# The gate as a tanh of half its argument, and a new order for the first third of a written-out list of steps

## The chip, the cores and the metric

The kernel runs on one core of one Trainium2 chip. The metric is the time of one launch in microseconds of the device; three runs of the kernel before took 293.01, 293.01 and 293.41 us, a median of 293.01 us.

## The reference

For 8 batches, 8 heads, 576 tokens and 64 channels a head, the reference computes a linear attention and feeds it to a gated layer. All is in float32.

```python
q_s = softmax(q, over the 64 channels of a head)
k_s = softmax(k, over the 576 tokens)
kv  = einsum('bhsd,bhse->bhde', k_s, v)          # 64x64 a head
x   = q_s @ kv, heads side by side               # (576, 512) a batch
gate = sigmoid(sum over 5 taps of conv_w[t] * x shifted by 4 - t tokens)   # per channel
out = (gate * (x @ w_val)) @ w_out
```

## The kernel before, in words

The 512 channels lie on the 128 partitions in four blocks, the 576 tokens along the free axis. The work is cut into named steps, one small function each, with a batch and a block as arguments: `tap 0 1 3` is the step `tap` (L546) of batch 0, block 1, tap 3. `ORDER` (L32) is a list of 969 steps written out by hand; the kernel walks down it and issues each step's instructions, so the list is the order on every engine's queue at once. A letter at a step's end names its engine (`a` ScalarE, `v` VectorE, `p` GpSimd). Nothing else moves an instruction: an engine takes its own steps in the order of the list and waits at each for what the step needs. All loads and stores (`load_*`, `put`, `k_row`, `k_spread`) are issued by SyncE, also in list order.

The steps of a batch, with the engine that does them:

- k: batches 0 and 1 load k by channels (`load_kc`, L314), take the maximum (`k_top`, VectorE), the exponential (`k_raise`, ScalarE) and turn it on TensorE (`k_turn`, `k_tail_turn`, copied out by `k_turned`, `k_tail_turned`). Later batches load it by tokens, take the maximum from a second copy (`load_km`, `k_peak`), spread it over the partitions through memory (`k_row`, `k_spread`), subtract it on GpSimd (`k_sub`, L298) and take the exponential (`k_exp`, `kt_exp`).
- q: maximum (`q_max`), subtraction (`q_sub`, GpSimd) and exponential (`q_exp`; `q_each` does both on ScalarE, eight heads one by one), sum (`q_sum`, with `q_eps` and `q_rec`), scaling (`q_mul`), turned on TensorE (`q_turn`, `tail_turn`, copied out by `q_turned`, `tail_turned`, `tail_high`).
- `kv`, `kv_sums`, `kv_norm`, then `attend`, which writes x of two blocks at a time into PSUM.
- the gate of one block: `first` scales x by the newest tap, `tap` adds one of the four others on VectorE straight from PSUM, or else `far` (ScalarE) writes the scaled block to SBUF and `near` (GpSimd) adds it; then `sigmoid` (L560).
- `x_high` and `x_low` split x in a rounded part and the rest; `value` (L584) multiplies both by the weights in 24 matmuls of 288 columns a half; `gated` (L588) multiplies the result in PSUM by the gate; `g_high`, `g_low` split that; `project` (L600) multiplies it by the second weights; `copy` (L609) brings it out of PSUM and `put` stores it.
- the weights arrive as 64-bit words and are converted once, in eight slabs (0 to 3 of `w_val`, with the conv taps, 4 to 7 of `w_out`): `part`, `field`, `scaled`, `signed`, `joined`, `taps`, `w_high`, `w_low`. `value b m` needs slab m, `project b n` slab 4 + n.

PSUM is cut into four equal buffers under one tag (`bank`, L152). Each of the four x blocks, each `value` and `project`, `kv` and each group of turned blocks takes one, and a new one takes the buffer whose last reader stands earliest in the list. SBUF tiles are shared in the same way (six buffers for k's second copies and the weights in conversion, two for stored output, two each for q, k and v).

ScalarE's functions need tables; the compiler puts an ACT_TABLE_LOAD ahead of an ACTIVATE whose function the tables in place do not have.

Of the kernel before, what the change touches and what calls it, by code (L numbers as in the profile page):

```python
# [51 lines left out]
    k_tail_turn 1, k_turn 1 1, field 7 p, first 0 2 a, q_eps 1 2 4 a, k_turned 1 0 a, tap 0 2 3, q_rec 1 2 4,
    k_tail_turned 1 a, q_rec 1 0 2, tap 0 3 3, w_high 4 a, q_mul 1 3 p, value 0 2, k_peak 2 0, g_high 0 1 a,
    q_mul 1 1 p, g_high 0 0 a, tap 0 3 2, k_turned 1 1 a, tap 0 2 2, q_mul 1 2 p, w_high 5 a, tap 0 3 1, g_low 0 0 p,
    q_mul 1 0 a, k_peak 2 3, kv 1, tap 0 2 1, k_row 2, g_low 0 1 p, tap 0 2 0, scaled 7 a, scaled 6 a, tap 0 3 0,
    w_low 5 p, sigmoid 0 2, q_turn 1 0, k_peak 3 3, load_k 2, load_kt 2, kv_sums 1, value 0 3, part 6 p, part 7 a,
    load_km 3 1, gated 0 2, kv_norm 1 a, load_vt 2, q_max 2 0 5, k_spread 2, g_high 0 2 p, q_turned 1 0 a, w_low 4 p,
    sigmoid 0 3, g_low 0 2 p, q_turn 1 1, gated 0 3, attend 1 0, signed 7, g_high 0 3 a, q_turned 1 1 a, signed 6,
    x_high 1 0 a, g_low 0 3 v, project 0 0, first 1 0 a, first 1 1 a, joined 6 p, tap 1 0 3, x_high 1 1 a, tap 1 0 2,
    joined 7 p, project 0 1, tap 1 0 1, copy 0 0 a a, w_high 6 a, put 0 0, x_low 1 0, w_high 7 a, load_km 3 0,  # L60
    w_low 6 p, tap 1 0 0, load_km 4 1, tap 1 1 3, w_low 7 p, load_km 5 0, tap 1 1 2, load_v 2, attend 1 1, copy 0 1 a a,
# [623 lines left out]
```

## Time and profile before

The profile is of one execution. Its span, first to last instruction, is 291.0 us; the launch takes about 2.0 us more (293.01 - 291.0).

| engine | busy us | share of the span | instructions |
|---|---|---|---|
| TensorE matmuls | 264.8 | 91% | 2544 |
| VectorE | 235.7 | 81% | 332 |
| ScalarE | 219.1 | 75% | 339 |
| GpSimd | 203.5 | 70% | 190 |

In 40 slices of the span (7.3 us each) TensorE is at nine tenths or more in all but the first six and the last; the first two are empty, the fourth and fifth are at seven and three tenths. VectorE, ScalarE and GpSimd are at seven to nine tenths from the second slice on. A group of instructions is a line of the kernel, an engine, an operation and its tiles, with the count, the busy time, the mean duration of one, and the idle time of the engine ahead of them with what ended it. Starts in a timeline are from the start of the span, and durations of neighbours on one engine overlap a little, so what one costs its engine is the distance from start to start.

### The profile page before, as it was taken

The numbers are of one execution on the slowest core, as the hardware profiler recorded it, in microseconds if no ns is written. First come the engines' busy times: TensorE is split into PE (matmuls) and PEld (weight loads), VectorE is DVE, ScalarE is ACT, GpSimd is POOL, SyncE is SP. The second block draws the span as 40 slices with busy tenths as digits, with TensorE's granted clock in tenths as the row PEclk, the third lists the DMA queues.
The fourth block names the chain that finished last, engine by engine and source line by source line (L and its number), as shares of the span: only waits on it lengthen the run. The fifth ranks groups of instructions, "written<-read, shape, count | busy, mean of one in ns | idle before, by whom it ended". The sixth has DMA issues, their size and how long they took to land.

```text
span 291.0 us, 6460 instructions
## 1 busy us (share of the span) xinstructions
PE 264.8 (91%) x2544; PEld 249.0 (86%) x2544; DVE 235.7 (81%) x332; ACT 219.1 (75%) x339; POOL 203.5 (70%) x190
## 2 busy tenths in 40 slices
...
GB/s 228 399 415 402 360 334 4 279 140 328 353 137 331 219 174 317 273 264 207 184 276 339 252 111 322 385 166 118 147 187 138 199 35 2 41 41 83 0 83 81
DMA packets 22158, 60.77 MB, mean 209 GB/s; under 512 B 3184, under 2 KB 3696, under 8 KB 19440
## 3 DMA queue, kind: packets, MB, share of 16 engines
...
## 4 chain that ended last, share of the span: by engine, by line
PE 84%; DVE 6%; ACT 4%; DMA 2%; SPq 1%; issue 1%; ACTq 0%
PE out L572 36%; PE val L572 33%; PE kv L466 6%; PE x L525 5%; DMA kc<-in_k_channels 2%; PE qTps L491 2%; ACT q L444 1%; DVE qs L376 1%; DVE qm L361 1%; DVE ktop L322 1%; DVE e L258 1%; DVE e L257 1%; ACT L561 0%; DVE kpk L286 0%; ACT gate L561 0%
## 5 line engine op out<-in xcount | busy, mean ns | idle before, releaser
L572 PE MATMUL val<-x,w_val_hi 128*128 128x288 f32 x512 | 90.6, 299 | 0.0
L549 DVE SCALAR_TENSOR_TENSOR gate<-x,cw,gate 128x574 f32<-128x574 f32 (+3 forms) x107 | 85.3, 806 | 5.0 <-ACT gate L538 1.9
L572 PEld LDWEIGHTS val<-x,w_val_hi 128*128 128x128 f32 x512 | 76.9, 192 | 0.0
L572 PE MATMUL val<-x,w_val_lo 128*128 128x288 f32 x256 | 57.1, 305 | 5.6 <-DVE gate L549 5.6
L572 PE MATMUL out<-gh,w_out_lo 128*128 128x288 f32 x256 | 56.8, 301 | 0.0
L572 PE MATMUL out<-gh,w_out_hi 128*128 128x288 f32 x256 | 55.5, 296 | 0.0
L572 PEld LDWEIGHTS val<-x,w_val_lo 128*128 128x128 f32 x256 | 41.7, 192 | 6.9 <-POOL w_val_lo L274 6.0
L572 PEld LDWEIGHTS out<-gh,w_out_lo 128*128 128x128 f32 x256 | 41.0, 188 | 5.8 <-issue 2.2
L598 POOL TENSOR_TENSOR gl<-g,gh 128x576 fp32r<-128x576 f32 x22 | 31.4, 1429 | 16.7 <-ACT gh L166 9.7
L166 ACT COPY o<-out 128x576 f32<-128x576 f32 (+1 forms) x29 | 17.9, 621 | 32.2 <-PE out L572 23.4
L572 PEld LDWEIGHTS out<-gh,w_out_hi 128*128 128x128 f32 x256 | 41.2, 188 | 0.0
L558 POOL TENSOR_TENSOR gate<-gate,far 128x572 f32<-128x572 f32 (+3 forms) x21 | 28.0, 1339 | 18.7 <-ACT far L554 10.8
L572 PE MATMUL out<-gl,w_out_hi 128*128 128x288 f32 x256 | 39.5, 295 | 0.0
L572 PEld LDWEIGHTS out<-gl,w_out_hi 128*128 128x128 f32 x256 | 35.9, 188 | 0.0
L590 DVE TENSOR_TENSOR g<-val,gate 128x576 f32<-128x576 f32 x32 | 24.1, 754 | 14.2 <-PE val L572 10.2
L366 POOL TENSOR_TENSOR q<-q,qm 128x512 f32<-128x512 f32 x31 | 32.3, 1063 | 2.4 <-issue 2.4
L301 POOL TENSOR_TENSOR k<-k,kmax 128x512 f32<-128x512 f32 x23 | 30.4, 1339 | 0.2
L544 DVE TENSOR_TENSOR x<-x,x 128x576 fp32r<-128x576 f32 x32 | 23.3, 749 | 2.9 <-ACT x L166 1.6
L435 POOL TENSOR_TENSOR qc<-qc,lb 128x576 f32<-128x576 f32 x13 | 19.1, 1480 | 8.9 <-DMA lb<-lrow 5.8
L561 ACT ACTIVATE gate<-gate 128x576 f32<-128x576 f32 x32 | 21.5, 684 | 0.9 <-DVE gate L549 0.6
L554 ACT ACTIVATE far<-x,cw 128x572 f32<-128x572 f32 (+3 forms) x21 | 15.4, 740 | 8.5 <-PE x L525 3.2
L166 ACT CAST x<-x 128x576 fp32r<-128x576 f32 x27 | 17.0, 642 | 6.0 <-PE x L525 4.3
...
## 6 DMA issues: line engine op xcount, KB each, us to landing
...
```

The costliest lines, as they stand in the source:

```text
L166: nc.scalar.copy(out=out, in_=in_)
L301: engine(e).tensor_sub(kk[r, cs], kk[r, cs], mx[r, cs])
L366: engine(e).tensor_tensor(qq, qq, m, op=ALU.add if b < 2 else ALU.subtract)
L435: engine(e).tensor_sub(t, t, T["lb", b][:, p])
L466: nc.tensor.matmul(acc[h * D:(h + 1) * D, p, :], T["k", b][:, c, cs] if c < 4 else ktz[b % 2][:, cs], T["v", b][:, c, hd] if c < 4 else T[ ...
L544: nc.vector.tensor_sub(xl, T["x", b, p], T["xh", b, p].bitcast(F32))
L549: nc.vector.scalar_tensor_tensor(out=a, in0=x, scalar=w, in1=a, op0=ALU.mult, op1=ALU.add)
L558: nc.gpsimd.tensor_add(a, a, T["far", b, p, j])
L561: nc.scalar.activation(T["gate", b, p], T["gate", b, p], AF.Sigmoid)
L572: nc.tensor.matmul(ps[:, cs], a[:, kb, ms], z[:, cs], start=(i == 0), stop=(i == len(parts) - 1))
L590: nc.vector.tensor_mul(T["g", b, m], T["val", b, m], T["gate", b, m])
L598: engine(e).tensor_sub(T["gl", b, m], T["g", b, m], T["gh", b, m].bitcast(F32))
```

## The change

Three functions: the gate becomes tanh(x/2) instead of sigmoid(x); `gated` multiplies the value by gate + 1 in one instruction with two operations instead of one multiplication; `copy` scales by 0.5 where it only copied. Together that is the same product. In `ORDER` the steps ahead of `q_mul 2 3 p` (317 before, 320 after) stand in another order, some on another engine, and three of batch 0's and 1's taps (`tap 0 1 2`, `tap 0 0 0`, `tap 1 0 0`) become a `far` and a `near` each. The first 22 loads keep their order. From `q_mul 2 3 p` on the two lists are the same, step by step (the diff shows some of these lines only for their line breaks).

```diff
-    load_words 3, load_q 0 2 5, load_q 0 1 2, load_words 0, load_kc 0 0, load_kc 0 2, load_ident, load_kc 0 3, part 3 a,
...
-    q_sub 0 1 p, q_exp 0 3 4, k_raise 0 2, k_top 0 3, part 0 p, load_km 2 2, load_words 2, k_raise 0 3, signed 0,
-    q_exp 0 2 3, k_top 0 1, k_raise 0 0, field 1 p, q_sum 0 2 5, q_exp 0 1 2, joined 0 p, k_raise 0 1, k_turn 0 0,
-    part 1 a, load_km 2 1, load_kc 1 0, load_kc 1 2, load_q 1 0 5, load_words 5, scaled 1 p, q_max 0 0 1, q_eps 0 2 5 p,
-    k_turn 0 1, signed 1, q_each 0 0, load_kc 1 3, q_rec 0 2 5, k_turned 0 0 v, q_mul 0 4 p, k_tail_turn 0,
-    k_turned 0 1 a, q_mul 0 3 p, q_sum 0 0 2, tail_turn 0, k_tail_turned 0 a, taps 3 p, joined 1 v, tail_turned 0 a,
-    kv 0, w_high 0 a, q_eps 0 0 2 v, field 2 p, q_rec 0 0 2, k_peak 2 2, tail_high 0 a, q_mul 0 1 a, q_mul 0 0 p,
-    k_top 1 0, k_peak 2 1, q_mul 0 2 p, q_turn 0 0, k_top 1 2, w_high 3 a, scaled 2 p, kv_sums 0, taps 1 a, taps 0 a,
-    part 2 p, q_turn 0 1, kv_norm 0 v, q_turned 0 0 a, signed 2, q_turned 0 1 a, attend 0 0, q_max 1 0 2, joined 2 p,
-    k_raise 1 2, attend 0 1, q_max 1 2 4, w_high 1 p, field 5 p, first 0 1 a, x_high 0 0 a, tap 0 1 3, first 0 0 a,
-    q_sub 1 0 p, k_top 1 3, x_high 0 1 a, taps 2 p, tap 0 0 3, w_low 1 p, k_raise 1 3, tap 0 1 2, scaled 5 a,
-    w_high 2 a, part 5 p, load_km 3 2, load_kc 1 1, load_words 4, load_words 6, load_k 4, load_km 2 0, x_low 0 1,
-    load_v 1, x_high 0 2 a, w_low 3 p, tap 0 1 1, x_high 0 3 a, k_raise 1 0, tap 0 1 0, q_sub 1 1 p, load_km 2 3,
...
-    k_top 1 1, w_low 2 p, tap 0 0 0, x_low 0 2, field 4 p, q_exp 1 0 1, x_low 0 3, value 0 1, k_raise 1 1, signed 5,
...
+    load_words 3, load_q 0 2 5, load_q 0 1 2, load_words 0, field 3 p, part 3 a, load_kc 0 0, scaled 3 a, signed 3,
...
+    load_words 1, q_sum 0 2 5, load_q 0 0 1, taps 3 p, scaled 0 a, q_sub 0 1 p, k_raise 0 2, k_top 0 1, k_top 0 3,
+    load_vt 0, q_exp 0 1 2, load_v 0, load_km 2 2, k_raise 0 0, load_words 2, q_eps 0 2 5 a, w_low 3 p, q_rec 0 2 5,
+    k_raise 0 1, k_turn 0 0, field 1 p, k_raise 0 3, part 1 p, q_max 0 0 1, load_km 2 1, scaled 1 a, k_turn 0 1,
+    signed 1, joined 1 v, q_each 0 0, k_turned 0 0 a, q_mul 0 4 p, k_tail_turn 0, q_sum 0 0 2, tail_turn 0, signed 0,
+    taps 1 p, load_kc 1 0, k_tail_turned 0 a, q_eps 0 0 2 a, q_rec 0 0 2, q_mul 0 2 p, tail_turned 0 v,
+    k_turned 0 1 a, load_kc 1 2, field 2 p, load_q 1 0 5, q_mul 0 1 a, q_mul 0 0 p, scaled 2 a, q_mul 0 3 p,
+    part 2 a, kv 0, q_turn 0 0, q_turn 0 1, tail_high 0 a, joined 0 p, k_top 1 0, k_peak 2 2, k_top 1 2, kv_sums 0,
+    q_turned 0 0 a, kv_norm 0 v, load_words 5, signed 2, attend 0 0, load_kc 1 3, load_km 3 2, joined 2 p,
+    q_turned 0 1 a, first 0 1 a, far 0 1 2, q_max 1 0 2, x_high 0 1 a, q_max 1 2 4, attend 0 1, field 5 p, k_top 1 3,
+    x_high 0 2 a, taps 2 p, taps 0 p, tap 0 1 3, x_high 0 0 a, load_km 2 3, tap 0 1 0, w_high 1 p, x_high 0 3 a,
+    first 0 0 a, w_high 0 p, q_each 1 3, load_kc 1 1, w_low 1 p, x_low 0 1, w_high 2 p, tap 0 1 1, x_low 0 0,
+    x_low 0 2, tap 0 0 2, first 0 3 a, load_v 3, first 0 2 a, q_sub 1 0 p, tap 0 0 1, w_low 0 p, tail_high 1 a,
+    k_raise 1 3, load_words 4, scaled 5 p, q_sub 1 1 p, near 0 1 2, k_raise 1 0, x_low 0 3, tap 0 0 3, far 0 0 0,
+    tap 0 2 2, value 0 1, load_v 1, load_words 6, load_words 7, q_exp 1 0 1, sigmoid 0 1, value 0 0, k_top 1 1,
+    w_low 2 p, k_raise 1 1, tap 0 2 1, q_exp 1 1 2, gated 0 1, near 0 0 0, k_turn 1 0, tap 0 2 3, field 4 p,
+    tap 0 2 0, load_km 2 0, scaled 4 p, k_raise 1 2, q_sum 1 0 2, signed 4, load_k 2, q_each 1 2, signed 5,
+    sigmoid 0 0, field 7 p, value 0 2, part 4 a, g_high 0 1 a, q_eps 1 0 2 a, gated 0 0, k_turned 1 0 a, q_rec 1 0 2,
+    k_tail_turn 1, q_sum 1 2 4, g_high 0 0 a, part 5 p, tap 0 3 2, q_eps 1 2 4 a, joined 4 p, value 0 3, sigmoid 0 2,
...
+    k_turn 1 1, load_q 2 0 5, k_peak 2 3, q_mul 1 3 p, g_low 0 1 p, joined 5 p, gated 0 2, q_mul 1 2 a, field 6 p,
+    tap 0 3 1, g_high 0 2 a, k_turned 1 1 a, q_turn 1 0, q_turned 1 0 a, scaled 7 a, q_max 2 0 5, part 6 a,
+    k_peak 2 1, kv 1, kv_sums 1, kv_norm 1 v, w_high 5 a, q_turn 1 1, g_low 0 2 p, sigmoid 0 3, attend 1 0,
...
-        nc.scalar.activation(T["gate", b, p], T["gate", b, p], AF.Sigmoid)
+        nc.scalar.activation(T["gate", b, p], T["gate", b, p], AF.Tanh, scale=0.5)
...
-        nc.vector.tensor_mul(T["g", b, m], T["val", b, m], T["gate", b, m])
+        nc.vector.scalar_tensor_tensor(out=T["g", b, m], in0=T["gate", b, m], scalar=1.0, in1=T["val", b, m], op0=ALU.add, op1=ALU.mult)
...
-        copied(e, T["o", b, n][:, piece(h)], T["out", b, n][:, piece(h)])
+        times(e, T["o", b, n][:, piece(h)], T["out", b, n][:, piece(h)], 0.5)
```

## Rows read from the trace of the kernel before

**Rows 1.** The waits of the whole span: engine and line, releaser, us in total, times, longest.

```profile
PE kps L333 <- ACT kc L326: 14.9, 1, 14.9
PE val L572 <- DVE gate L549: 5.6, 1, 5.6
PE ktps L345 <- DVE g L590: 0.6, 1, 0.6
```

**Rows 2.** Two stretches: length, busy us of PE, PEld, DVE, ACT, POOL, granted clock, DMA.

```profile
30.00:40.00 10.00, 6.31 (x29) 6.34 (x30) 9.93 (x15) 9.98 (x26) 8.49 (x10) 0.66 0.96 366
...
50.00:60.00 10.00, 10.00 (x125) 9.14 (x122) 9.90 (x14) 8.53 (x20) 7.70 (x8) 1.00 0.62 215
```

**Rows 3.** The chain that ended last: start us, us, what.

```profile
57.74 6.60 PE out L572 x48
...
287.37 0.40 ACT o L166
```

**Rows 4.** Timeline of PE: start us, us, line, operation, tiles, count, idle time before.

```profile
25.96 2.17 PE L525 MATMUL x<-qT,kvd 64*64 64x288 f32 x32 [0.23 <-ACT qT L166]
33.69 0.82 PE L572 MATMUL val<-x,w_val_lo 128*128 128x288 f32 x2 [5.56 <-DVE gate L549]
...
39.37 0.43 PE L572 MATMUL val<-x,w_val_lo 128*128 128x288 f32 x2
...
81.60 0.69 PE L466 MATMUL kv<-v,k 128*64 128x65 f32 x16
```

**Rows 5.** Timeline of DVE, to the release of x's first buffer.

```profile
5.22 0.43 DVE L176 TENSOR_SCALAR e<-e 128x517 f32<-128x517 f32 x1 [5.22 <-POOL e L248]
...
10.40 1.52 DVE L322 TENSOR_REDUCE ktop<-kc 128x1 f32<-128x576 f32 x2 [1.24 <-DMA kc<-in_k_channels]
...
18.22 1.16 DVE L168 COPY k<-kps 128x1024 f32<-128x1024 f32 x1
...
21.39 0.70 DVE L286 TENSOR_REDUCE kpk<-km 128x1 f32<-128x576 f32 x1
...
31.89 2.37 DVE L549 SCALAR_TENSOR_TENSOR gate<-x,cw,gate 128x573 f32<-128x573 f32 x3
```

**Rows 6.** Timeline of ACT: the first gate, and the exponential of batch 2's k.

```profile
38.99 1.28 ACT L561 ACT_TABLE_LOAD   x1
40.29 0.69 ACT L561 ACTIVATE gate<-gate 128x576 f32<-128x576 f32 x1
...
77.00 1.91 ACT L305 ACTIVATE k<-k 128x2048 f32<-128x2048 f32 x1
```

**Rows 7.** Groups of ACT, shapes apart: count, busy us, mean ns, idle before.

```profile
L561 ACT ACT_TABLE_LOAD x14 | 18.0, 1283 | 2.6 <-DVE gate L549 2.4
L326 ACT ACTIVATE kc<-kc,ktop 128x576 f32<-128x576 f32 x8 | 6.2, 774 | 0.2 <-DVE ktop L322 0.2
L166 ACT CAST w_out_hi<-f 128x512 fp32r<-128x512 f32 x4 | 2.4, 621 | 0.0
L172 ACT ACTIVATE e<-e 128x512 f32<-128x512 f32 x4 | 2.4, 618 | 0.0
```

**Rows 8.** Timeline of POOL, from the last weights to batch 2's k.

```profile
58.92 3.00 POOL L261 TENSOR_TENSOR f<-e,f 128x512 int32<-128x512 int32 x2 [2.15 <-DVE e L258]
62.42 2.55 POOL L274 TENSOR_TENSOR w_out_lo<-f,w_out_hi 128x512 fp32r<-128x512 f32 x2 [0.50 <-ACT w_out_hi L166]
...
72.44 3.82 POOL L301 TENSOR_TENSOR k<-k,kmax 128x512 f32<-128x512 f32 x3
```

**Rows 9.** Groups of DVE and POOL, shapes apart, for `gated`, `tap` and `near`.

```profile
L590 DVE TENSOR_TENSOR g<-val,gate 128x576 f32<-128x576 f32 x32 | 24.1, 754 | 14.2 <-PE val L572 10.2 <-POOL gl L598 2.1 <-ACT kvd L485 1.3
L549 DVE SCALAR_TENSOR_TENSOR gate<-x,cw,gate 128x575 f32<-128x575 f32 x29 | 23.4, 807 | 3.0 <-ACT gate L538 1.9 <-ACT x L166 1.0
...
L558 POOL TENSOR_TENSOR gate<-gate,far 128x574 f32<-128x574 f32 x6 | 7.2, 1208 | 7.0 <-DVE gate L549 5.0 <-ACT far L554 2.1
L558 POOL TENSOR_TENSOR gate<-gate,far 128x575 f32<-128x575 f32 x3 | 4.7, 1568 | 2.2 <-ACT far L554 2.1
```

More of the change, by code (lines that the diff above doesn't have):

```diff
@@ L52 @@
[L52 to L61, printed above, removed]
@@ new lines @@
+    x_high 1 2 a, x_high 1 3 a, tap 1 1 2, tap 1 1 1, tap 1 1 0, q_sub 2 0 p, first 1 3 a, q_sub 2 4 p, q_sub 2 3 p,
+    q_sub 2 2 p, tap 1 1 3, q_sub 2 1 p, project 0 2, load_km 4 3, load_kt 2, x_low 1 3, x_low 1 2, k_peak 3 2,
+    tap 1 3 2, put 0 0, copy 0 2 a a, put 0 1, value 1 1, load_q 3 0 5, w_low 7 p, k_peak 4 1, near 1 0 0,
+    first 1 2 a, k_peak 3 0, load_km 4 0, project 0 3, k_sub 2 0 p, k_sub 2 2 p, load_km 3 3, sigmoid 1 1, gated 1 1,
+    k_sub 2 3 p, tap 1 2 3, value 1 0, q_exp 2 0 5, load_k 4, q_sum 2 0 5, load_km 5 0, k_peak 3 3, copy 0 3 a a,
@@ L71 @@
-    tail_turn 2, value 1 2, q_sub 3 3 p, tap 1 2 0, load_q 4 0 5, tail_turned 2 a, tail_high 2 a, k_peak 4 3,
-    load_km 5 2, sigmoid 1 2, g_low 1 0 v, q_turned 2 1 a, g_low 1 3 v, attend 2 0, gated 1 2, q_exp 3 0 4, k_peak 4 0,
-    g_high 1 2 p, k_peak 4 2, g_low 1 2 p, project 1 0, x_high 2 0 v, k_row 4, first 2 1 a, q_sum 3 0 4, far 2 0 3,
-    k_sub 3 0 p, x_high 2 1 a, k_sub 3 4 p, project 1 3, copy 1 0 a a, tap 2 1 3, first 2 0 a, put 1 0, q_eps 3 0 4 p,
-    load_km 5 1, far 2 0 2, tap 2 1 2, near 2 0 3, x_low 2 1, tap 2 1 1, k_sub 3 2 p, project 1 1, copy 1 3 a a,
@@ L76 @@
-    q_rec 3 0 4, tap 2 1 0, far 2 0 0, put 1 3, near 2 0 2, q_max 4 0 5, load_vt 6, kt_exp 3, k_sub 3 3 p, attend 2 1,
-    copy 1 1 a a, k_sub 3 1 p, tap 2 0 1, put 1 1, project 1 2, load_km 6 2, first 2 2 a, x_low 2 0, q_mul 3 1 p,
-    k_spread 4, x_high 2 3 a, x_high 2 2 a, q_mul 3 2 p, tap 2 2 3, q_sub 4 4 p, x_low 2 2, sigmoid 2 1, tail_high 3 p,
-    q_sub 4 3 p, first 2 3 a, copy 1 2 a a, x_low 2 3, value 2 1, near 2 0 0, put 1 2, tap 2 2 2, load_km 6 0, load_v 4,
-    k_peak 5 3, q_sub 4 1 p, k_exp 3, value 2 0, gated 2 1, load_qc 4 3, q_mul 3 0 p, tap 2 3 3, g_high 2 1 a,
@@ L91 @@
[L91 to L93 removed]
+    kv_norm 2 v, load_qc 4 1, q_turn 2 1, tap 1 2 1, k_spread 3, q_turned 2 0 a, q_sub 3 2 p, load_km 5 3,
+    k_peak 5 0, tail_turn 2, value 1 2, q_sub 3 3 p, tap 1 2 0, load_q 4 0 5, tail_turned 2 a, tail_high 2 a,
@@ new lines @@
+    k_peak 4 3, load_km 5 2, sigmoid 1 2, g_low 1 0 v, q_turned 2 1 a, g_low 1 3 v, attend 2 0, gated 1 2,
+    q_exp 3 0 4, k_peak 4 0, g_high 1 2 p, k_peak 4 2, g_low 1 2 p, project 1 0, x_high 2 0 v, k_row 4, first 2 1 a,
+    q_sum 3 0 4, far 2 0 3, k_sub 3 0 p, x_high 2 1 a, k_sub 3 4 p, project 1 3, copy 1 0 a a, tap 2 1 3,
+    first 2 0 a, put 1 0, q_eps 3 0 4 p, load_km 5 1, far 2 0 2, tap 2 1 2, near 2 0 3, x_low 2 1, tap 2 1 1,
+    k_sub 3 2 p, project 1 1, copy 1 3 a a, q_rec 3 0 4, tap 2 1 0, far 2 0 0, put 1 3, near 2 0 2, q_max 4 0 5,
```

121 lines of the change are left out of this document (62 added, 59 removed).

## The prediction

> **What bounds the kernel now.** I read the chain that ended last first: from the 57.74 us of its first `project` to the last copy at 287.37 every piece of it is TensorE's [rows 3]. The waits say where TensorE stood still: 14.9 us for its first operand, 5.6 us at the first `value`, 0.6 us at `k_tail_turn 1` about 44 us, and none of its matmuls after that [rows 1]; in the stretch from 50 to 60 us it is busy for all of it [rows 2]. So the kernel is a head of some 45 us, in which TensorE is fed by the others, and 243 us of matmuls end to end. Nothing done to ScalarE, VectorE or GpSimd in the second part can shorten it; it can only lengthen it. The time is settled by when the matmuls become continuous. The reader is to compare from here on when the first `project` starts, 57.74 [rows 3], since the matmuls ahead of it (four `value`, the turns and kv of batch 1, one `attend`) are the same in both lists.
>
> The timeline of TensorE shows the head's last gap: `attend` of batch 0 ends at 28.1 (25.96 + 2.17), `value 0 1` starts at 33.69 after 5.56 of idling, released by a tap on VectorE [rows 4]. That tap is not an operand of `value`. The four x blocks hold all four PSUM buffers, and `value 0 1` waits for the last reader of block 1, `tap 0 1 0`, the second of the three taps that start at 31.89 [rows 5]. VectorE is busy for 9.93 of the 10 us from 30 to 40 [rows 2]: its work up to that tap sets the start.
>
> **What the new list does to that start.** The last reader of block 1 in the list is now `tap 0 1 1`. Of VectorE's steps ahead of it, against those ahead of `tap 0 1 0` before, there leave: the copy `k_turned 0 0` (1.16 and a little overlap, 1.1) and `k_peak 2 1` (0.70, so 0.65), both [rows 5]; `tap 0 1 2`, now a `far` and a `near`, and `tap 0 0 3`, now later (0.79 each by the three in 2.37 [rows 5], 0.75 from start to start); `q_eps`, about 0.1. Together 3.35. `tail_turned 0` comes in, half the size of that copy: 0.55. Net 2.8 less. `scaled 3` leaves VectorE too (0.43 at 5.22), but it is a link of the chain from the first weights to `signed 3`, and ScalarE does it in about the same time at the same moment: nothing. Behind it VectorE still stands until the k load lands at 10.40 [rows 5].
>
> Two waits come in on VectorE's in-order queue. `signed 1` needs `scaled 1`, now behind two `k_raise` (0.774 each [rows 7], 0.67 from start to start) that cannot begin before `k_top 0 1`; walking down both queues VectorE is there at 15.6 and the operand at 16.2. `q_sum 0 0 2` then waits some 0.2 for `q_each 0 0`. Behind both stands all of VectorE's chain. They cost between nothing, if the walk is off by that much, and 1.5, two steps late; I take 0.7 net. So `value 0 1` starts at 33.69 - 2.8 + 0.7 = 31.6, a gain of 2.1. Its slab of weights (`w_low 1`) is done near 30.2 by the same walk along GpSimd, and `attend` ends near 27.4, so neither is the last to come.
>
> **From there to the first `project`.** Before: 57.74 - 33.69 = 24.05, of which 0.6 is idle [rows 1, 3, 4]. The new order has the same matmuls, 23.45. What comes late in it: `k_tail_turn 1` needs the buffer that `gated 0 0` empties; on ScalarE `q_each 1 2` now stands ahead of `sigmoid 0 0`, on VectorE `signed 4` and `signed 5` ahead of `gated 0 0`, which ends near 44, when TensorE arrives near 44.5; `kv 1` waits about 0.4 for `k_turned 1 1`. I put 0.5 there (bounds 0 and 2, one `q_each`). First `project`: 31.6 + 23.95 = 55.5, a gain of 2.2.
>
> **The gate itself.** Before, the first gate pays a table load of 1.28 at 38.99 [rows 6], and ScalarE has 14 such loads ahead of gates, 18.0 us in all [rows 7], hidden but for the first, since TensorE does not wait. The new list sets exponentials between gates (`q_exp 1 1 2`, `k_raise`, `q_each 1 2` between `sigmoid 0 1` and `sigmoid 0 0`). Whether tanh shares the tables of the exponential no row shows: the price is nothing, or a load at every change. Copies and scalings stand among both kinds with no load of their own [rows 7], so sharing happens; I take nothing, and the other end is a rival below.
>
> The trace has the gate start at 40.29, 0.02 after its load ended: a change costs 1.30 here [rows 6]. The Trainium skill ("ScalarE: Activation LUTs", What ACT_TABLE_LOAD costs) puts 2.66 on a change, a drain of about 1.38 included. By that the first gate would have 1.4 more to win; the row shows no such drain, and the sum goes by the row.
>
> `gated` becomes an instruction of the taps' kind with the same two operand places: 807 against 754 ns [rows 9], 0.05 x 32 = 1.7 us of VectorE over the run. VectorE stands 10.2 us ahead of `gated` waiting for `value` [rows 9], which hides it; without that cover it would cost up to 1.7. `copy` with a factor: a scaling and a copy of one size take 618 and 621 ns on ScalarE [rows 7], so the last one, 0.40 at 287.37 [rows 3], gains or loses under 0.05.
>
> **Is the lead kept?** The next date is `kv 2`, at 81.60 before [rows 4], which needs `k_exp 2`, 77.00 to 78.91 [rows 6], and that GpSimd's last `k_sub 2`, done at 76.26 (72.44 + 3.82) [rows 8]. GpSimd comes to that from `joined 6`, which waited 2.15 for VectorE's `signed 6` and started at 58.92 [rows 8]. By VectorE's list `signed 6` ends again near 58.6: x and the gates come earlier, but `x_high 1 0` (0.65) and `kv_norm 1` are new on that queue ahead of it. After `joined 6` GpSimd's work is the same but for `near 1 0 0`, 1.2 to 1.57 [rows 9], against a wait of 0.50 that goes [rows 8]. So `k_exp 2` ends near 79.3 at the earliest, and TensorE is there at 81.6 - 2.2 = 79.4. There is no slack left, but no loss either. From `q_mul 2 3 p` on the lists agree, and VectorE, 2.3 us of work lighter by then, keeps pace.
>
> Sum: 291.0 - 2.2 = 288.8 of span, and with the 2.0 us around it (the runs' median 293.01 less 291.0) 290.8.
>
> **Rivals.**
> (a) The lead is given back at batch 2. Should `signed 6` or a `k_sub` be a microsecond or two late, `kv 2` starts that much late, and the unchanged rest was paced for the old start. For it: VectorE at 9.90 of 10 us in 50 to 60 [rows 2] and GpSimd's chain without slack. Against it: the chain begins no later than before, so it can take the lead and hardly more. With 1.5 lost: 292.3.
> (b) More is won. From 33.69 TensorE ran at half its clock: two matmuls start to end take 0.82 at 33.69 and 0.43 at 39.37 [rows 4], granted 0.66 on average from 30 to 40 [rows 2], so 1.2 GHz and then 2.4; it had idled for 5.6 before. Now it idles for about 4.2. If the clock stays up, `value 0 1` takes 3.2 and not 5.7, but `gated 0 0` then holds `k_tail_turn 1`, and 0.6 is left of the 2.5; with the two new VectorE waits gone as well, 289.5.
> (c) Slower: tanh has other tables than the exponential. Then `sigmoid 0 1`, the `k_raise` after it and `sigmoid 0 0` each pay 1.30, 3.9 ahead of `gated 0 0`, where TensorE has 0.5 of slack: 3.4 lost against 2.2 won, 294.2. It decides from the second load on. For it: each change between exponential and gate pays in the trace [rows 6, 7]. Against it: nothing in a row of this case.
>
> The Trainium skill ("ScalarE: Activation LUTs", Table sets: the hidden batching unit) lists tanh in the set of the exponential, and no run here shows it. By that page alone (c) falls away.
>
> **How the numbers follow.** As forecast 0.47, (a) 0.28, (b) 0.13, (c) 0.12. The forecast's own range, by the bounds of the VectorE waits and of the 0.5: 289.8 to 291.9. Over all cases 289.2 to 293.0: outside lie (c), part of (a) and a little of (b). What can be told from no change is about 0.2%, 0.6 us. Faster by more: the forecast, (b) and 0.17 of (a), 0.77. Within: 0.07 of (a). Slower: (c) and 0.04 of (a), 0.16.
>
> **What the profile after would show.** `value 0 1` starting near 31.6, behind `tap 0 1 1`; the first `project` near 55.5; no table load between exponential and gate, so ACT_TABLE_LOAD left only beside the logarithm; `gated` at 0.80 to 0.81; `kv 2` near 79.4, with no wait of TensorE after it. A wait of TensorE on ScalarE's `k_exp` or VectorE after 55 us speaks for (a), a granted clock at full through 30 to 40 for (b), loads at the line of the gate for (c). A first `project` after 57 would make the prediction wrong at its root.

## The result, and the profile after

The changed kernel takes 296.53 us in the median of four runs (294.98 to 297.86), against 293.11 for the kernel before beside it: a ratio of 1.0114 with a 95% interval of 1.0094 to 1.0134. It is slower; 290.8 was forecast. The profiled execution took 295.62 us, with a span of 293.8.

The dates that the prediction went by, read as starts on TensorE's timeline (the first `project` stands 0.07 earlier there than in the chain of waits, 57.67 for 57.74 before):

| kernel | `value 0 1` | first `project` | `kv 2` | `kv 5` to `kv 6` | end of matmuls | ratio to before, interval |
|---|---|---|---|---|---|---|
| before | 33.69 | 57.67 | 81.60 | 37.38 | 287.29 | |
| after | 32.62 | 57.23 | 83.35 | 38.43 | 290.08 | 1.0114, 1.0094 to 1.0134 |
| functions alone | 34.36 | 58.32 | 82.25 | 38.45 | 289.01 | 1.0039, 1.0024 to 1.0054 |
| list alone | 32.86 | 62.62 | 91.29 | 37.39 | 299.42 | 1.0333, 1.0298 to 1.0368 |

The end of the matmuls moved by 2.79. By stretches: `value 0 1` is 1.07 earlier; from there to the first `project` it takes 0.63 more (24.61 for 23.98); from the first `project` to `kv 2`, 2.19 more (26.12 for 23.93); from `kv 5` to `kv 6`, 1.05 more; the rest is unchanged. The gain at `value 0 1` is half of what was forecast, and three losses stand behind it: a smaller one up to the first `project`, and two in stretches where I had none.

TensorE's waits after (engine and line, releaser, us in total, times, longest), against [rows 1]:

```profile
PE val L575 <- DVE gate L552: 4.3, 1, 4.3
PE kv L469 <- ACT q L454: 1.5, 1, 1.5
...
PE qTps L494 <- DVE g L593: 0.6, 1, 0.6
...
PE out L575 <- DVE gh L171: 0.4, 1, 0.4
```

The wait at `value` fell as forecast (5.6 before), and the other three shown are new; those at `kv` and at `project` lie behind 55 us, where TensorE waited for nothing before. The chain of waits after, start, us and what:

```profile
57.30 6.60 PE out L575 x48
63.90 1.44 PE x L528 x13
65.33 0.48 ACT x L169
65.81 5.34 DMA out<-o
...
72.42 0.69 ACT gate L564
73.11 2.25 ACT q L373
75.38 2.82 DVE qs L379
...
83.35 2.55 PE kv L469 x80
```

Before, every piece from 57.74 on was TensorE's [rows 3]. Now the chain leaves TensorE at 65.3 and runs through a store, ScalarE's `q_exp 2` and VectorE's `q_sum 2`, until `kv 2`. The store is the place to look. SyncE's own timeline after, then of the kernel before (issue time, us, what is loaded or stored):

```profile
57.62 0.33 SPq L294 DMA_DIRECT2D krow<-kpk  x1
...
65.81 0.90 SPq L618 DMA_DIRECT2D out<-o  x2
...
72.57 0.42 SPq L218 DMA_DIRECT2D v<-in_v  x1
```

```profile
49.26 0.33 SPq L291 DMA_DIRECT2D krow<-kpk  x1
...
61.85 0.34 SPq L615 DMA_DIRECT2D out<-o  x1
...
64.12 0.43 SPq L215 DMA_DIRECT2D v<-in_v  x1
```

`k_row 2`, the first transfer of this part, goes out 8.4 us later than before: it needs `k_peak 2 0`, which the new list sets behind `gated 0 3`. `put 0 0` goes out 4.0 later and `load_v 2` 8.5 later. These two have their own reason, their places in the new list: `put 0 0` stands behind a load that waits 2.6 us for GpSimd's `w_low`, and `load_v 2` stands where `load_v 3` stood, behind loads that wait 2.7 for a `k_peak` and 0.8 for another `w_low`, while `load_v 3` now goes out near 25 us. (A kernel below has `k_row 2` as late as here, and no wait at `kv 2`.) The DMA engines' share is the next to last column of the windows (length, busy us of PE, PEld, DVE, ACT, POOL, granted clock, DMA share, GB/s); the window from 50 to 60 is to be held against the same one of [rows 2], 0.62 there:

```profile
30.00:40.00 10.00, 7.06 (x41) 6.88 (x42) 9.93 (x15) 9.57 (x22) 9.75 (x11) 0.83 1.02 416
50.00:60.00 10.00, 9.02 (x137) 7.78 (x136) 9.67 (x15) 9.98 (x20) 7.99 (x7) 1.00 0.11 7
60.00:70.00 10.00, 10.00 (x82) 9.15 (x81) 9.82 (x15) 5.32 (x9) 8.87 (x9) 1.00 0.89 271
```

The DMA engines are nearly idle in that window (0.11) and nearly full in the next (0.89). ScalarE after (start, us, line, operation, tiles, idle time before and what ended it): the first gate, the third copy, the exponential of batch 2's k.

```profile
37.96 0.68 ACT L564 ACTIVATE gate<-gate 128x576 f32<-128x576 f32 x1
...
71.25 0.65 ACT L175 ACTIVATE o<-out 128x576 f32<-128x576 f32 x1 [4.12 <-DMA out<-o]
...
79.53 1.91 ACT L308 ACTIVATE k<-k 128x2048 f32<-128x2048 f32 x1
```

`copy 0 2` writes into a buffer that `put 0 0` has to empty first (there are two), and stands 4.12 us for it; everything behind it on ScalarE is late, `k_exp 2` by 2.5 [rows 6]. `load_v 2`, issued at 72.57 and landing 10.6 later, near 83.2, is the last operand of `kv 2`, which starts at 83.35; `k_exp 2` has ended by 81.44. VectorE and GpSimd after:

```profile
16.62 0.73 DVE L260 TENSOR_SCALAR e<-e 128x517 int32<-128x517 int32 x1 [0.62 <-ACT e L175]
...
29.43 1.67 DVE L552 SCALAR_TENSOR_TENSOR gate<-x,cw,gate 128x575 f32<-128x575 f32 x2 [0.38 <-POOL w_val_hi L171]
...
43.67 1.78 DVE L261 SCALAR_TENSOR_TENSOR e<-words,e 128x512 int32<-128x512 int32 x1
45.38 0.74 DVE L593 SCALAR_TENSOR_TENSOR g<-gate,val 128x576 f32<-128x576 f32 x1
...
56.85 0.75 DVE L289 TENSOR_REDUCE kpk<-km 128x1 f32<-128x576 f32 x1
...
60.36 0.69 DVE L261 SCALAR_TENSOR_TENSOR e<-words,e 128x512 int32<-128x512 int32 x1
```

```profile
43.61 1.29 POOL L264 TENSOR_TENSOR f<-e,f 128x512 int32<-128x512 int32 x1 [1.59 <-ACT f L175]
...
61.13 2.56 POOL L264 TENSOR_TENSOR f<-e,f 128x512 int32<-128x512 int32 x2 [3.06 <-DVE e L261]
```

The second half of `signed 5` takes 1.78 beside GpSimd's `joined 4`, where the same instruction takes 0.69 at 60.36. `k_peak 2 0` is the row at 56.85, and `k_row 2` goes out behind it. `joined 6` starts at 61.13, against 58.92 before [rows 8]. Last the groups of table loads and of `gated` (count, busy us, mean ns), against [rows 7, 9]; with one more at each of two other lines, nine loads are left of the 33 before:

```profile
L402 ACT ACT_TABLE_LOAD x4 | 5.1, 1283 | 0.1
L564 ACT ACT_TABLE_LOAD x3 | 3.8, 1283 | 0.0
...
L593 DVE SCALAR_TENSOR_TENSOR g<-gate,val 128x576 f32<-128x576 f32 x32 | 24.0, 750 | 16.2 <-PE val L575 12.3 <-ACT gate L564 2.3 <-ACT kvd L488 1.3
```

The gates load tables three times, and the logarithm (L402) four: tanh shares the tables of the exponential, as (c) doubted.

### The profile page after: what moved, and what is told of

Read it like the earlier page. It is cut to its first block, busy times and chain, and to the rows that moved or that the text cites. A ratio compares the mean times of both kernels' runs of the same rounds, so it can differ in the third digit from the quotient of the medians.

```text
span 293.8 us, 6438 instructions
## 1 busy us (share of the span) xinstructions
PE 265.6 (90%) x2544; PEld 248.6 (85%) x2544; DVE 236.1 (80%) x329; ACT 191.0 (65%) x318; POOL 204.9 (70%) x190
## 3 DMA queue, kind: packets, MB, share of 16 engines
q1 hardware_dynamic: 22128, 60.36, 61.2%
## 4 chain that ended last, share of the span: by engine, by line
PE 73%; DVE 10%; ACT 8%; DMA 5%; issue 3%; SPq 1%; ACTq 0%; DVEq 0%
PE out L575 33%; PE val L575 28%; PE x L528 6%; PE kv L469 5%; DVE qs L379 3%; DMA kc<-in_k_channels 3%; DVE gate L552 2%; DMA out<-o 2%; ACT q L454 2%; PE qTps L494 1%; ACT q L373 1%; ACT gate L564 1%; DVE x L547 1%; ACT qT L169 1%; ACT kc L329 1%
## 5 line engine op out<-in xcount | busy, mean ns | idle before, releaser
L552 DVE SCALAR_TENSOR_TENSOR gate<-x,cw,gate 128x575 f32<-128x575 f32 (+3 forms) x104 | 83.4, 808 | 5.5 <-ACT gate L541 1.9
L575 PEld LDWEIGHTS val<-x,w_val_hi 128*128 128x128 f32 x512 | 75.9, 190 | 0.0
L561 POOL TENSOR_TENSOR gate<-gate,far 128x572 f32<-128x572 f32 (+3 forms) x24 | 31.6, 1320 | 19.2 <-ACT far L557 11.5
L175 ACT ACTIVATE o<-out 128x576 f32<-128x576 f32 (+1 forms) x29 | 18.3, 635 | 39.8 <-PE out L575 24.2
L593 DVE SCALAR_TENSOR_TENSOR g<-gate,val 128x576 f32<-128x576 f32 x32 | 24.0, 750 | 16.2 <-PE val L575 12.3
L304 POOL TENSOR_TENSOR k<-k,kmax 128x512 f32<-128x512 f32 x23 | 31.0, 1368 | 0.2
L557 ACT ACTIVATE far<-x,cw 128x572 f32<-128x572 f32 (+3 forms) x24 | 17.7, 741 | 11.6 <-PE x L528 4.3
L547 DVE TENSOR_TENSOR x<-x,x 128x576 fp32r<-128x576 f32 x32 | 23.2, 749 | 1.7 <-ACT x L169 1.6
L541 ACT ACTIVATE gate<-x,cw 128x576 f32<-128x576 f32 x26 | 19.2, 748 | 4.3 <-PE x L528 4.1
```

The lines of the kernel that those rows point to most:

```text
L175: nc.scalar.mul(out, in_, factor)
L304: engine(e).tensor_sub(kk[r, cs], kk[r, cs], mx[r, cs])
L541: nc.scalar.activation(a, x, AF.Copy, scale=w)
L547: nc.vector.tensor_sub(xl, T["x", b, p], T["xh", b, p].bitcast(F32))
L552: nc.vector.scalar_tensor_tensor(out=a, in0=x, scalar=w, in1=a, op0=ALU.mult, op1=ALU.add)
L561: nc.gpsimd.tensor_add(a, a, T["far", b, p, j])
```

## The experiments

Positions are starts of TensorE in the profiled execution.

### The two halves of the change

The old list with the three new functions:

```diff
-        nc.scalar.activation(T["gate", b, p], T["gate", b, p], AF.Sigmoid)
+        nc.scalar.activation(T["gate", b, p], T["gate", b, p], AF.Tanh, scale=0.5)
...
```

> The old list with the new functions (tanh, the two-operation product, the scaled copy). If the new list is the cause of the loss, this is not slower than before: 291.7 to 293.2, since one table load of 1.28 us ahead of the first gate goes and all the others were hidden. If the functions are the cause (ScalarE running ahead without table loads, so that GpSimd and VectorE meet at other moments in the unchanged part), it is 295 or more, and TensorE has waits after 100 us.

Measured: 294.53 us, 1.0039 (1.0024 to 1.0054). The head is no shorter without the table load of the first gate [rows 6]: from `value 0 1` to the first `project` 23.96, against 23.98. It began 0.67 later, the first k load landing at 11.06 and not 10.40 [rows 5]: a matter of the start-up, which the functions don't touch (in the three kernels further below with the same functions and the list the same up to batch 4, that load lands at 10.09 to 10.64, and `value 0 1` starts 23.2 to 23.3 behind it, as here and as before). And the stretch from `kv 5` to `kv 6` took 38.45: the loss of 1.05 belongs to the functions.

The new list with the old functions, sigmoid and all:

> The new list with the old functions (sigmoid, with its table loads). If the list is the cause, this is as slow as the changed kernel or slower, 296 to 300, since two or three table loads of 1.28 us come between the exponentials and the gates of batch 0 as well. If the functions are the cause, it is 291 to 294.

Measured: 303.27 us, 1.0333 (1.0298 to 1.0368); `kv 5` to `kv 6` 37.39. Of TensorE's waits:

```profile
PE kv L468 <- ACT k L307: 3.9, 1, 3.9
PE ktps L347 <- ACT k L168: 3.4, 1, 3.4
```

That is slower than the 296 to 300 expected. The list sets gates between exponentials and needs the tanh; with table loads between them the first `project` is 5.4 later than after. Of that 3.4 is at the place that (c) gave, `k_tail_turn 1`, and of its size, though ScalarE's `k_turned 1 0` ended that wait and not `gated 0 0`; the 3.9 at `kv 2` (behind `k_exp 2`) (c) did not have. So list and functions do not add: 1.0333 and 1.0039, but 1.0114 together.

### SyncE's queue

The changed kernel with `load_v 3` and `load_v 2` in exchange (the early one takes the free buffer):

```diff
-    x_low 0 2, tap 0 0 2, first 0 3 a, load_v 3, ...
+    x_low 0 2, tap 0 0 2, first 0 3 a, load_v 2, ...
```

> The changed kernel with the loads of v of batches 2 and 3 exchanged in the list, so that v of batch 2 is loaded at 25 us and not at 72.6. If kv of batch 2 waits for that load, its wait of 1.46 us at 83.35 goes and the time falls by 1.0 to 1.6, kv 2 starting near 82. If it waits for ScalarE, as the view of waits names it, nothing changes (within 0.5).

The changed kernel with the first two stores right behind the copies that fill them, ahead of the loads that wait for GpSimd's weights:

```diff
-    copy 0 1 a a, attend 1 1, ... copy 0 0 a a, ... load_km 4 3, load_kt 2, ... put 0 0, copy 0 2 a a, put 0 1,
+    copy 0 1 a a, put 0 1, attend 1 1, ... copy 0 0 a a, put 0 0, ... load_km 4 3, load_kt 2, ... copy 0 2 a a,
```

> The changed kernel with the first two stores each right behind its copy in the list, ahead of the loads of k's second copies that now hold them up. If ScalarE's 4.1 us of waiting for the first store's end matters, q_exp of batch 2 starts near 69 and not 73, and the time falls by 0.2 to 1.0 (what kv 2 loses besides its v). If only the load of v sets kv 2, the wait goes and the time stays within 0.4.

Measured: 295.47 us, 1.0080 (1.0064 to 1.0096) and 295.18, 1.0095 (1.0058 to 1.0131). First `project` to `kv 2`: 25.38 and 25.61, against 26.12; each alone wins little. Both together:

> The changed kernel with both changes to SyncE's queue: v of batch 2 loaded before that of batch 3, and the first two stores right behind their copies. If the queue's order is what costs 2.2 us between the first project and kv of batch 2, that stretch falls from 26.1 to 24.0 to 24.6, and the time by 1.4 to 2.2. If ScalarE and GpSimd are late of themselves by then, it stays at 25 or more.

Measured: 294.11 us, 1.0033 (1.0019 to 1.0047); the stretch is 24.18 (23.93 before). A row of ScalarE from the kernel with the exchange, one of TensorE from that with the stores, and two of ScalarE from that with both:

```profile
71.78 0.65 ACT L174 ACTIVATE o<-out 128x576 f32<-128x576 f32 x1 [4.61 <-DMA out<-o]
```

```profile
82.89 0.69 PE L468 MATMUL kv<-v,k 128*64 128x65 f32 x16 [1.37 <-ACT q L453]
```

```profile
69.02 0.65 ACT L174 ACTIVATE o<-out 128x576 f32<-128x576 f32 x1 [1.61 <-issue]
...
78.06 1.90 ACT L307 ACTIVATE k<-k 128x2048 f32<-128x2048 f32 x1
```

And one of SyncE from that with both:

```profile
57.90 0.33 SPq L293 DMA_DIRECT2D krow<-kpk  x1
```

With the exchange alone `copy 0 2` still waits for the store, and `k_exp 2` for it. With the stores alone `kv 2` still waits for v (the releaser named is ScalarE's scaling of q, which `kv` doesn't read; v lands then). Only with both gone is `copy 0 2` at 69.02 and TensorE without a wait at `kv 2`. Two waits lay one behind the other, and taking one away uncovers the next. This is the larger loss: 1.94 of the 2.19; the other 0.25 stays open. `k_row 2` is no earlier in that kernel (57.90), and the DMA share is 0.09 from 50 to 60 us and 0.84 and 0.97 in the two stretches behind it, much as after. So a late `k_row 2` and idle DMA engines are not enough for the loss; the places of the stores and of `load_v 2` in the list made it.

### What the missing table load does between kv 5 and kv 6

VectorE's `g_high 4 3` and `g_low 4 3`, and GpSimd beside them, before:

```profile
186.48 0.46 DVE L168 CAST gh<-g 128x576 fp32r<-128x576 f32 x1
186.98 0.76 DVE L598 TENSOR_TENSOR gl<-g,gh 128x576 fp32r<-128x576 f32 x1
```

```profile
187.18 1.84 POOL L558 TENSOR_TENSOR gate<-gate,far 128x575 f32<-128x575 f32 x1 [1.59 <-ACT far L554]
```

And with the functions alone, where ScalarE has no table load of 1.28 ahead of `far 5 0 3`:

```profile
187.14 1.02 DVE L169 CAST gh<-g 128x576 fp32r<-128x576 f32 x1
188.20 1.73 DVE L599 TENSOR_TENSOR gl<-g,gh 128x576 fp32r<-128x576 f32 x1
```

```profile
186.42 1.43 POOL L559 TENSOR_TENSOR gate<-gate,far 128x575 f32<-128x575 f32 x1 [0.19 <-ACT far L555]
187.81 3.26 POOL L302 TENSOR_TENSOR k<-k,kmax 128x512 f32<-128x512 f32 x2
```

Before, VectorE starts first and GpSimd's `near 5 0 3` is long, 1.84 for 1.43. Now GpSimd starts first and VectorE is long, by 0.56 and 0.97, with `project 4 0` waiting 0.38 and 0.17 and taking 4.37 from its start to the `attend` behind it (186.08 to 190.45), where it took 3.36 before (185.42 to 188.78). The theory: ScalarE done earlier sends GpSimd ahead of VectorE, and the one that comes second waits for the other's instruction to end. The ends fit: 186.42 + 1.43 + 0.46 = 188.31, and `g_high` ends at 188.16; before, 186.98 + 0.76 + 1.43 = 189.17, and `near` ends at 189.02; in the head of the changed kernel 43.61 + 1.29 + 0.69 = 45.59, and `signed 5` ends at 45.45. The Trainium skill ("SBUF — State Buffer", SBUF: two separate sides) says that VectorE, in a two-port mode or with two inputs from SBUF, and GpSimd share a pair of ports, which the one that starts first holds for its whole instruction while the other blocks. The traces of this case agree, to 0.15 us in each of the three.

Three kernels test it, all the old list with the new functions. Work put back on ScalarE, two exponentials done twice, about the time of the table load:

```diff
-    g_low 4 1 p, c_exp 5 2, c_exp 5 3, gated 4 3, ...
+    g_low 4 1 p, c_exp 5 2, c_exp 5 3, c_exp 5 2, c_exp 5 3, gated 4 3, ...
```

> The old list with the new functions, and the two exponentials c_exp 5 2 and c_exp 5 3 done twice over: 1.26 us of work more on ScalarE, about what the table load ahead of them was, and the same values. If the functions cost 1.07 us between kv of batches 5 and 6 because ScalarE, without that load, lets GpSimd's near start 1.3 us earlier and run beside VectorE's g_high and g_low of the last block of batch 4, those two fall from 1.02 and 1.73 us back to 0.46 and 0.76, and the kernel is FASTER for the added work by 0.8 to 1.1 us, near 293.5. If not, it is the same or slower, 294.5 to 295.8.

Measured: 293.47 us, 1.0026 (1.0015 to 1.0038). That is the 293.5 expected, but by luck: the stretch is 38.13, so only 0.32 came back, and the rest of the difference to 294.53 is an earlier start (`value 0 1` at 33.40, not 34.36). VectorE and GpSimd:

```profile
186.19 0.46 DVE L170 CAST gh<-g 128x576 fp32r<-128x576 f32 x1
186.69 1.96 DVE L600 TENSOR_TENSOR gl<-g,gh 128x576 fp32r<-128x576 f32 x1
```

```profile
186.61 1.43 POOL L560 TENSOR_TENSOR gate<-gate,far 128x575 f32<-128x575 f32 x1 [1.34 <-ACT far L556]
```

The delay missed by 0.08: `near` still starts just ahead of `g_low`, which then takes 1.96. Next, `g_low 4 3` on GpSimd, ahead of `near`:

```diff
-    far 5 0 3, g_high 4 3 v, g_low 4 3 v, project 4 0, ...
+    far 5 0 3, g_high 4 3 v, g_low 4 3 p, project 4 0, ...
```

> The old list with the three new functions, and g_low 4 3 on GpSimd instead of VectorE. Theory (without the gate's table load ScalarE is early, so GpSimd's near 5 0 3 and k_sub fall beside VectorE's g_high 4 3 and g_low 4 3, which are stretched from 0.46 and 0.76 to 1.02 and 1.72 us, and project 4 3 waits for them): GpSimd now does g_low ahead of near, nothing runs against it, and the stretch from kv 5 to kv 6 comes back from 38.45 to 37.4 to 37.7 us; time about 0.8 us under that of the old list with the new functions (294.5), 293.4 to 293.9. Rival (project 4 3 waits for something else, an earlier dead time of ScalarE's or a load): the stretch stays at 38.3 to 38.6, the time at 294.3 to 294.7. Second rival (GpSimd is itself late at that place): the stretch grows beyond 38.6, TensorE waiting on GpSimd's gl.

Measured: 293.45 us, 1.0022 (1.0012 to 1.0031); the stretch is 37.93 (37.4 to 37.7 expected), so half came back. GpSimd needs 1.43 for what VectorE does in 0.76, and `project` now waits for it (0.25). Last, `g_low` kept on VectorE and `near` made later, by setting `far 5 0 3` behind a `g_high 4 3` on ScalarE:

```diff
-    c_exp 5 3, gated 4 3, first 5 0 a, far 5 0 3, g_high 4 3 v, g_low 4 3 v, ...
+    c_exp 5 3, gated 4 3, first 5 0 a, g_high 4 3 a, far 5 0 3, g_low 4 3 v, ...
```

> The old list with the three new functions; g_high 4 3 goes from VectorE to ScalarE, and far 5 0 3 stands behind it there, so that GpSimd's near 5 0 3 starts after VectorE's g_low 4 3. Theory (the loss between kv 5 and kv 6 is GpSimd's work beside VectorE's g_low): g_low takes 0.76 again and not 1.72, TensorE doesn't wait for it, and the stretch is 37.4 to 37.6 us (38.45 with the old list and new functions, 37.38 before); the time is 1 us below the 294.5 of that kernel if it starts alike, and a ratio of 0.999 to 1.001 to the kernel before if it starts as that one. Rival (the stretch is lost elsewhere): 38.1 to 38.6. Second rival (near 5 0 3 and the k_sub behind it are now late on GpSimd): g_low at 0.76, and a wait of TensorE behind near or k_exp 6.

```profile
187.10 0.76 DVE L599 TENSOR_TENSOR gl<-g,gh 128x576 fp32r<-128x576 f32 x1 [0.74 <-ACT gh L167]
```

Measured: `g_low` at 0.76, `near` behind it at 187.79, the stretch 37.62, and 293.26 us, 1.0007 (0.9999 to 1.0016). That is the whole loss of the functions but 0.24 (`project 4 0` now waits 0.27 for `g_high 4 3`, which is later on ScalarE), and it settles the cause.

### The head

In the changed kernel, `signed 5` set behind `gated 0 0` (the edit below); and, by itself, `joined 4` taken from GpSimd and set on VectorE behind `gated 0 0`:

```diff
-    q_each 1 2, signed 5, sigmoid 0 0, ... gated 0 0, ...
+    q_each 1 2, sigmoid 0 0, ... gated 0 0, signed 5, ...
```

> The changed kernel with signed 5 moved behind gated 0 0 on VectorE. signed 5 takes 2.2 us there, its second half 1.78 where its like takes 0.69. If VectorE's queue ahead of gated 0 0 is what holds TensorE at 45 to 46 us, gated 0 0 starts near 43.3 and not 45.38, and the first project near 56.2 and not 57.23 (0.5 to 1.2 earlier). If another engine's work is as late, it moves by less than 0.3.

> The changed kernel with joined 4 taken from GpSimd and done on VectorE behind gated 0 0; the order ahead of gated 0 0 stays. If signed 5 is long because GpSimd's joined 4 runs beside it, both reading two operands from SBUF, its second half falls from 1.78 to about 0.69 and gated 0 0 starts near 44.3, the first project 0.3 to 1.0 earlier. If signed 5 is long for another reason, it stays at 1.78 and VectorE is 0.6 later behind it.

Measured: 295.49 us, 1.0102 (1.0083 to 1.0121), first `project` 57.09; and 295.13, 1.0078 (1.0063 to 1.0094), 56.91, with `signed 5`'s second half back at 0.69 and `gated 0 0` at 44.44 instead of 45.38. In the first the clash only moved, to `signed 5`'s first half (1.31). `value 0 1` starts at 32.69 and 32.79 there, against 32.62, so from it to the first `project` they take 24.40 and 24.12, against 24.61: without the clash the head is 0.5 shorter, with the 0.69 that `joined 4` takes on VectorE in it. Then `signed 5` behind `gated 0 2`, first by itself, then with `joined 5` behind it too (the edit of the second):

```diff
-    q_mul 1 3 p, g_low 0 1 p, joined 5 p, gated 0 2, q_mul 1 2 a, ...
+    q_mul 1 3 p, g_low 0 1 p, gated 0 2, signed 5, joined 5 p, q_mul 1 2 a, ...
```

> The changed kernel with signed 5 behind gated 0 2 in the list. Theory (VectorE's in-order queue ahead of gated 0 2 and q_rec 1 2 4 holds q_turn 1 0, and so the first project): gated 0 0 starts at 43.2 to 43.6 instead of 45.38, gated 0 2 by 49.5, the first project at 55.7 to 56.3 instead of 57.23; the time falls by less than that, 0 to 0.8 (295.7 to 296.5), as the loads of batch 2 still set kv 2. Rival (ScalarE or GpSimd's share of q holds q_turn 1 0): first project at 56.9 to 57.3. Second rival (slab 5 is late for project 0 1): the first project is early, and a wait for the weights' e or w_out stands behind it.

> The changed kernel with signed 5 (VectorE) and behind it joined 5 (GpSimd) set behind gated 0 2. Theory (VectorE's queue ahead of gated 0 2 holds the head, and no step behind it is late): gated 0 2 done by 49.4 instead of 51.0, kv 1 at 51.4, VectorE's kv_norm 1 done by 54.8, the first project at 56.1 to 56.5 instead of 57.23; the time falls by 0 to 0.9, as put 0 0 and load_v 2 then bind as before. Rival (GpSimd is late with joined 5, and so slab 5's w_low for project 0 1): the first project stands at 56.9 to 57.3, with a wait for w_out. Second rival (ScalarE's q_mul 1 2 or k_turned 1 1 holds kv 1 whatever VectorE does): kv 1 at 51.9 or later, the first project at 56.8 to 57.2.

In the first I left `joined 5` ahead of `signed 5` in the list, so slab 5 of the weights is joined before its signs are set, and that kernel multiplies by other weights; `signed 5` waits for `joined 5` and VectorE stands 2.65. It tells little: 297.88 us, 1.0176 (1.0156 to 1.0196). The second: 295.53, 1.0094 (1.0077 to 1.0111), and the first `project` at 57.69, no earlier. `kv 1` does start at 51.33, but TensorE then waits 1.66 at `attend 1 0`, which starts at 56.56, for `kv_norm 1`, whose last instruction is the third here:

```profile
49.78 1.78 DVE L260 SCALAR_TENSOR_TENSOR e<-words,e 128x512 int32<-128x512 int32 x1
...
52.21 2.80 DVE L363 TENSOR_REDUCE qm<-q 128x40 f32<-128x2560 f32 x1
...
55.99 0.42 DVE L484 TENSOR_TENSOR kvd<-kv,ks 128x256 f32<-128x256 f32 x1
```

The first row is `signed 5`'s second half: 1.78 again, now beside GpSimd's `g_low 0 1` (49.34 to 51.01). So this edit moved the clash and did not lift it. The 2.80 of `q_max 2 0 5` ahead of `kv_norm 1` looked like the cause. Moved behind `signed 6`, in the changed kernel:

> The changed kernel with one step moved: q_max 2 0 5 (2.80 us of VectorE) from ahead of kv_norm 1 to behind signed 6. Theory (this step in VectorE's queue holds kv_norm 1, k_peak 2 0 and with it SyncE's k_row 2, and signed 6 with GpSimd's joined 6): kv_norm 1 done at 55.0 to 55.3 instead of 55.95, k_row 2 issued near 56 instead of 57.62, joined 6 started near 59.5 instead of 61.13, put 0 0 earlier by some 1.5, kv 2 at 81.6 to 82.6 instead of 83.35; time 294.3 to 295.2. Rival (the loads behind load_km 4 3 and the late load_v 2 set kv 2, whatever VectorE does): kv 2 at 82.8 to 83.4, time 295.2 to 296. Second rival (q_max 2 is then late for q_sub 2): kv 2 later than 83.4.

Measured: 296.58 us, 1.0143 (1.0115 to 1.0172), `kv 2` at 84.24: the theory fell. VectorE stands 2.29 for `kv 1` in the gap, which `q_max` had been filling, and its work is then late, with TensorE waiting 1.24 and 0.79 between 65 and 72. The row of VectorE at `kv_norm 1`:

```profile
54.89 0.16 DVE L477 TENSOR_SCALAR ks<-kv 128x4 f32<-128x4 f32 x1 [2.29 <-PE kv L468]
```

So no single step of those tried holds the head. In the changed kernel VectorE is busy for 9.67 to 9.93 of each 10 us from 30 to 60 us, and where `signed 5` or `q_max 2 0 5` was moved back in its queue, a wait came up elsewhere.

### The parts together

> The changed kernel with signed 5 and joined 5 behind gated 0 2, load_v 3 and load_v 2 swapped, put 0 1 and put 0 0 right behind their copies, and g_low 4 3 on GpSimd. Theory (the parts add): first project at 56.1 to 56.5, kv 2 at 80.3 to 80.8 (81.60 before), kv 5 to kv 6 38.1, end of the matmuls at 286.7 to 287.2 (287.29 before); time 292.4 to 293.2, a ratio of 0.998 to 1.002. Rival (the loads of batch 2 are bound by the DMA engines whatever the head does): kv 2 stays at 81.4 to 81.8 however early the first project, and the time at 293.4 to 294.0.

> As the run before it in this call, but with VectorE's g_low 4 3 kept and near 5 0 3 made later (g_high 4 3 on ScalarE, far 5 0 3 behind it). Theory: as that run, and kv 5 to kv 6 at 37.4 to 37.6, so the matmuls end at 286.0 to 286.5 and the time is 291.7 to 292.5, a ratio of 0.995 to 0.999. Rival (loads bind kv 2): 292.7 to 293.3. Second rival (near 5 0 3 is late): the stretch stays at 38 or more and the time at that of the run before it.

> All parts together: signed 5 and joined 5 behind gated 0 2, q_max 2 0 5 behind signed 6, load_v 3 and load_v 2 swapped, put 0 1 and put 0 0 right behind their copies, g_high 4 3 on ScalarE with far 5 0 3 behind it. Theory: kv_norm 1 done by 54.9, the first project at 56.2 to 56.8 (57.83 without the move of q_max 2), kv 2 at 80.4 to 81.0, kv 5 to kv 6 37.6, end of the matmuls at 286.3 to 286.9 (287.29 before); time 292.0 to 292.6, a ratio of 0.996 to 0.999. Rival (GpSimd's w_low 5 holds the first project, or the loads of batch 2 hold kv 2): first project at 57.4 or later, or kv 2 at 81.5 to 82, and the time at 293.0 to 293.6.

Measured: 293.10 us, 1.0013 (1.0005 to 1.0022); 293.29, 1.0015 (1.0006 to 1.0023); 294.96, 1.0071 (1.0059 to 1.0084). (An earlier one, with the stores, the loads and `g_low 4 3` as in the first but `joined 5` left ahead of `signed 5`, took 296.74, 1.0133, 1.0105 to 1.0160; that fault is in it.) The first two lose 0.4 us where the changed kernel lost 3.3: the stores, the exchange of loads and the clash at `kv 6` are most of the loss. Their first `project` is at 57.91 and 57.83, `kv 2` at 81.92 and 81.83; the head missed what was expected of it (56.1 to 56.5), so it is by luck that the first one's time lies in its expected range. They end where the kernel before ends, not ahead of it, since the 1.07 at `value 0 1` is gone by the first `project`. The third has the shortest head of all: the first `project` at 56.89, 23.79 from `value 0 1`, where the kernel before takes 23.98. Moving `q_max 2 0 5` as well as `signed 5` and `joined 5` thus keeps a lead of 0.8 that far. But TensorE then waits 1.21 and 0.79 near 67 and 71 us, as it does with `q_max 2 0 5` moved alone and does not in the first two, and `kv 2` is at 83.92. No version beat the kernel before.

## Why the prediction was wrong

The span is 5.0 us longer than forecast, 293.8 for 288.8. 1.8 of it was lost by the first `project` (57.30 in the chain, 55.5 forecast), 2.15 more by `kv 2` (83.35, 79.4 forecast), and 1.05 between `kv 5` and `kv 6`. By its own sign, a first `project` after 57, the prediction was wrong at its root: the head won 0.44 and not 2.2. The other two turned those 0.44 into a loss; with both mended the kernel takes about what the kernel before takes (1.0013 and 1.0015). The forecast's own range, 289.8 to 291.9, is also narrower than the bounds that it cites: waits of 0 to 1.5 where 0.7 was taken, and 0 to 2 where 0.5 was, add up to 289.6 to 293.1.

- **What bounds the kernel, and the start.** Right in kind: `value 0 1` waits behind `tap 0 1 1`. It starts at 32.62, not 31.6. The wait of `signed 1` is there at the size given (0.62). Missing in the sum was a wait of 0.38 at 29.43 for GpSimd's `w_val_hi`. Some 0.6 of the 1.0 is not settled. The k load came 0.32 later (10.72), but with the same list it landed at 9.91 in the first run with `signed 5` behind `gated 0 2`, and `value 0 1` started at 32.64 all the same: VectorE then stood 0.53 for a `q_exp` and 0.78 for `signed 1`. `signed 0`'s second half was stretched from 0.69 to 1.07, but `signed 2`'s, 1.05 before, fell to 0.70.
- **To the first `project`.** This term was too small: 0.5 of waits were forecast, and 1.66 came. 0.35 came for `gated 0 0` (at `value 0 3`, which takes the buffer that it empties, not at `k_tail_turn 1`); 0.64 for `gated 0 2`, 0.35 at `attend 1 0` and 0.32 at 37.68 were not foreseen. The clash at `signed 5` is behind part of the first two: without it 0.5 came back. What holds the rest stays open. The clock came back earlier, part of what (b) had: 0.83 granted from 30 to 40 (0.66 before), pairs of matmuls at 0.43 from 35.60 on. Less the waits the stretch is 22.95, where the sum had 23.45, so the clock gave some 0.5 back (an estimate from these figures), and the waits took it. In the run with both SyncE edits the first pair took 0.50, but those from 34.13 on took 0.68 again (granted 0.77 from 35 to 40), and the stretch was the same 24.61. No run kept the clock up throughout, so what (b) is worth stays open.
- **Is the lead kept?** This step failed, and cost most: 2.15. It walked ScalarE, VectorE and GpSimd and left SyncE out, though `put`, `k_row` and all loads are issued by it in list order. `put 0 0` and `load_v 2`, set by the new list behind loads that wait, went out 4.0 and 8.5 later and set `kv 2` at 83.35 instead of 79.4. With both moved TensorE doesn't wait at `kv 2`, and 81.67 is the first `project`'s 57.49 and its matmuls. The chain that I did walk was off as well, by 2.4 at `signed 6` (61.05, not 58.6); with both moved `k_exp 2` ends at 79.96, early enough for 81.67, but 0.6 late had TensorE come at 79.4. Rival (a) named the place and gave it 1.5 of loss, with the argument that the chain could hardly take more than the lead.
- **The gate itself.** The price of tanh, of `gated` (750 ns, where 807 was assumed) and of the last copy was nothing, as said. "Hidden but for the first" was right that the loads hid, and wrong to stop there: one of them set which of two engines came first ahead of `kv 6`, and that cost 1.05. The first was hidden too: the head was as long without it.
- **"It can only lengthen it"** is in the prediction's first paragraph. Two changes off the path, in SyncE's order and in ScalarE's table loads, did just that, and my sum gave neither a term.
